# Routed attention and greedy experts on one core: one assignment product per block, split maxima in the first unit, copies on GpSimd, another order

## The chip, the cores and the metric

The kernel runs on one core of a Trainium2 chip. A core has TensorE (matrix products into PSUM), VectorE, ScalarE, GpSimd (elementwise work; GpSimd reaches SBUF only) and SyncE, which issues most of the DMAs; the profile calls them PE, DVE, ACT, POOL and SP. The metric is the device time of one execution in microseconds (us); smaller is better.

## The reference

Clustered attention feeds a layer of eight experts with a greedy, capacity-limited assignment.

```python
# q, k, v: (4, 8, 768, 64); centroids: (8, 16, 64)
q_assign = argmax(normalised(q) . normalised(c)); k_assign = argmax(normalised(k) . normalised(c))
mask = q_assign[:, :, :, None] == k_assign[:, :, None, :]
scores = where(mask, scale * q @ k.T, -1e9); scores -= max(scores, -1)
attn = exp(scores) / (sum + 1e-9);  x = (attn @ v) as (3072, 512)
logits = x @ w_gate                     # (3072, 8)
# all 24576 logits, largest first: give the token to the expert if it has none and the expert has < 384
out[mask_e] = relu(x[mask_e] @ w1[e]) @ w2[e]    # 8 experts, 512 -> 1024 -> 512
```

The argmax and the greedy order must come out as in float32, so the kernel splits most operands into a high and a low f16 part and adds their products.

## The kernel before

Attention is done in 8 units of four heads (`U = 8`, `HG = 4`); a head has 768 rows, six blocks of 128 (`J = 6`), so a unit has 24 blocks (`T = 24`). For every unit:

- `load` brings q, k and v in (SyncE's queue). `split_sc` (line 642) scales by 64, `split_hi` (646) makes the f16 high part and `split_lo` (650) the f16 remainder, called a residue here: on VectorE if its last argument is D, on GpSimd if it is P. `dup` (657) copies the high part into a second tile on ScalarE. `trans` (734) transposes by DMA on SyncE's queue; in unit 0 `pt` and `ptc` (738, 750) transpose on TensorE and copy out.
- `cent` (676) multiplies each of the 24 blocks with the unit's centroids. The centroids are also split in two, so `assign` (664) issues two matmuls of 16 columns per block, which add up in PSUM (tile `mx`). `hot0` to `hot5` (681, 697) turn the result into a one-hot mark on VectorE and write it with ScalarE beside q and k (+32768 for q, -32768 where k differs), so that a product of the marked operands is masked. Unit 0 does this head by head (`cent0`, `hh0` to `hh5`).
- `m_mm` (780) makes the masked scores of one block of queries, 2 x 384 columns, in a PSUM buffer `sc`; `m_rd` (787) takes the row maximum on VectorE. `row0` to `row2` put the maxima into the operand of the next product.
- `b_mm` (818) makes the transposed scores less the maximum, again in `sc`; `b_exp` (829) takes the exponential on ScalarE; `res` (835) makes the f16 residue of the weights, on GpSimd (P) or VectorE (D).
- `av` (850) multiplies with v: per block of 128 rows three matmuls of 66, 64 and 66 columns (`rest_of`, 840, is the third), and a fourth for the mean rows in one block of six. `out0` to `hi1` divide and split, `xst` stores, `xtr` transposes, `lg0` to `lg2` make the logits.

There are three buffers `sc`, shared by `m_mm`, `b_mm` and `pt`, and one buffer `mx`. Each engine works strictly in the order in which the instructions are issued to it, and that order is written out by hand: `ATT_ORDER` (22) is a text of some 2,050 steps such as `m_mm,3,5`, and a loop (1079) calls them one after the other. `wd` is a dummy product (671) that keeps TensorE busy, `tab,n` a step that fills a constant table (984), `tex` an exponential of one column (529) ahead of which the exponential table is loaded, `c2,n` the n-th operation of the centroids' norm (537), `bb` a first step of the routing. `FFN_ORDER` (186) does the same for routing and experts.

Of the kernel before, what the change touches and what calls it, by code (L numbers as in the profile page):

```python
# [21 lines left out]
tew teh ident load,0,q,0,A tex split_hi,0,q,0,D ones load,0,k,0 wtio wd loadc wd tab,0 misc wd tab,4 load,0,k,3 wd  # L22
load,0,k,2 wd load,0,k,1 wd load,0,q,1 split_lo,0,q,0,D load,0,q,2 pt,0,qa,0 c0 c1 load,0,v,- split_hi,0,k,0,D c2,0
load,1,k,- wd c2,1 wd c2,2 load,0,q,3 c2,3 split_sc,0,k,3 wd zkb split_lo,0,k,0,D loadg wd split_hi,0,k,3,P c2,4 wd c2,5
dup,0,k,3 c2,6 pt,0,ka,0 c2,7 split_sc,0,k,2 tab,18 c2,8 c2,9 split_hi,0,k,2,P wd c2,10 c2,11 wd split_sc,0,k,1 c2,12
c2,13 wd c2,15 c2,14 dup,0,q,0 wd ptc,0,qa,0,D c3 wd split_hi,0,k,1,P wd ptc,0,ka,0,D wd dup,0,k,1 wd split_lo,0,k,1,P
wd c4 wd dup,0,k,2 cent0,0,k split_sc,0,q,1 cent0,0,q split_lo,0,k,3,P wd split_sc,0,q,2 wd hh0,0 wd split_hi,0,q,1,P wd
hh1,0 pt,0,ka,1 tab,23 split_hi,0,q,2,P hh2,0 wd split_lo,0,q,1,P wd pt,0,ka,3 dup,0,k,0 hh3,0 dup,0,q,1 hh4,0,q hh4,0,k
split_lo,0,q,2,P pt,0,qa,1 ptc,0,ka,1,D hh5,0,k hh5,0,q wd wd split_sc,0,v,- ptc,0,qa,1,D cent0,1,k zqb tab,7 cent0,1,q
ptc,0,ka,3,D wd wd hh0,1 zqm wd split_hi,0,v,-,P pt,0,qb,0 hh1,1 pt,0,qa,2 split_lo,0,k,2,P hh2,1 pt,0,kb,0 hh3,1 wd wd  # L30
ptc,0,kb,0,D wd ptc,0,qb,0,A load,1,q,- split_lo,0,v,-,P hh4,1,q hh4,1,k ptc,0,qa,2,D split_sc,1,k,- m_mm,0,1 wd wd
m_rd,0,1 wd wd m_mm,0,0 split_sc,0,q,3 pt,0,ka,2 m_rd,0,0 m_mm,0,2 split_hi,0,q,3,P wd split_hi,1,k,-,P split_lo,0,q,3,P
m_rd,0,2 vs,0 load,1,v,- hh5,1,q split_lo,1,k,-,P ptc,0,ka,2,A wd pt,0,qb,1 wd vact,0 ptc,0,qb,1,D m_mm,0,3 vh2,0
m_mm,0,5 dup,0,q,3 vl2,0 wd wd hh5,1,k wd m_rd,0,3 dup,0,q,2 cent0,2,k cent0,2,q pt,0,kb,1 hh0,2 wd m_rd,0,5 wd
ptc,0,kb,1,A trans,1,ka,- wd wd pt,0,qa,3 split_sc,1,q,- wd hh1,2 m_mm,0,7 ptc,0,qa,3,D wd wd hh2,2 wd wd wd hh3,2 wd
split_hi,1,q,-,P m_mm,0,4 hh4,2,k hh4,2,q m_rd,0,7 cent0,3,k cent0,3,q wd hh5,2,q wd hh0,3 split_lo,1,q,-,P hh5,2,k wd
load,2,k,- m_rd,0,4 pt,0,qb,2 m_mm,0,6 ptc,0,qb,2,A wd wd hh1,3 wd m_rd,0,6 wd split_sc,1,v,- wd pt,0,kb,2 wd m_mm,0,9
hh2,3 wd hh3,3 wd wd ptc,0,kb,2,D wd wd trans,1,qa,- m_mm,0,8 hh4,3,q hh4,3,k hh5,3,q wd m_rd,0,9 split_hi,1,v,-,P
cent,1,k,0 cent,1,k,1 cent,1,k,2 m_rd,0,8 cent,1,k,3 wd hh5,3,k pt,0,qb,3 hot0,1,k m_mm,0,11 ptc,0,qb,3,A row1,0,0
row0,0,0 hot1,1,k pt,0,qm,0 m_rd,0,11 wd wd ptc,0,qm,0,A wd load,2,q,- wd wd pt,0,kb,3 hot2,1,k load,2,v,- dup,1,q,-  # L40
b_mm,0,0 ptc,0,kb,3,D m_mm,0,10 hot3,1,k wd wd m_rd,0,10 b_exp,0,0 wd wd wd m_mm,0,13 hot4,1,k res,0,0,P wd wd m_mm,0,12
m_rd,0,13 hot5,1,k cent,1,q,0 dup,1,k,- wd m_mm,0,14 m_rd,0,12 split_lo,1,v,-,P cent,1,q,1 cent,1,q,2 cent,1,q,3
m_rd,0,14 split_hi,2,k,-,D m_mm,0,15 trans,1,kb,- b_mm,0,2 m_rd,0,15 b_mm,0,1 b_exp,0,2 hot0,1,q m_mm,0,16 wd row0,0,1
b_exp,0,1 row1,0,1 wd hot1,1,q res,0,2,P wd pt,0,qm,1 m_rd,0,16 b_mm,0,3 ptc,0,qm,1,A hot2,1,q b_mm,0,5 res,0,1,P
b_exp,0,3 hot3,1,q wd m_mm,0,17 b_exp,0,5 hot4,1,q b_mm,0,4 split_lo,2,k,-,D hot5,1,q vs,1 split_hi,2,q,-,D trans,1,qb,-
wd m_rd,0,17 res,0,5,P m_mm,0,19 b_exp,0,4 wd m_rd,0,19 m_mm,0,18 b_mm,0,6 res,0,4,P m_rd,0,18 m_mm,0,20 b_exp,0,6
av,0,0 trans,2,ka,- m_mm,0,21 row1,0,2 row0,0,2 m_rd,0,20 b_mm,0,7 av,0,1 m_rd,0,21 b_exp,0,7 m_mm,0,22 split_hi,2,v,-,D
av,0,2 res,0,7,P m_rd,0,22 pt,0,qm,2 m_mm,0,23 b_mm,0,8 ptc,0,qm,2,A m_rd,0,23 tab,35 load,3,k,- res,0,3,P vact,1
b_mm,0,9 load,3,q,- vh2,1 b_exp,0,8 vl2,1 m_mm,1,0 av,0,3 m_rd,1,0 b_exp,0,9 res,0,8,P av,0,4 m_mm,1,1 av,0,5 m_rd,1,1
res,0,6,P b_mm,0,10 out0,0,0 m_mm,1,2 out1,0,0 b_exp,0,10 out2,0,0,D b_mm,0,11 res,0,9,P m_rd,1,2 hi0,0,0 cent,2,k,0  # L50
m_mm,1,4 b_exp,0,11 cent,2,k,1 cent,2,k,2 dup,2,k,- row1,0,3 tab,12 row0,0,3 hi1,0,0 res,0,10,P b_mm,0,13 m_rd,1,4
# [388 lines left out]
def routed_attention_greedy_moe(ctx: ExitStack, tc: tile.TileContext, q, k, v, centroids,  # L440
# [16 lines left out]
    BIG = 32768.0  # L457
    ER = 96
# [1080 lines left out]
```

## Time and profile before

| | |
|---|---|
| median of three runs | 676.03 us (675.4 to 678.72) |
| the profiled execution, its own time | 675.39 us |
| its span, first to last instruction | 673.6 us |
| TensorE / VectorE / ScalarE / GpSimd busy | 96% / 75% / 62% / 72% |
| mean granted TensorE clock | 0.978 of full speed |

The busy time of an engine is the time in which at least one of its instructions runs; matmuls overlap each other, so the distance from one start to the next tells more of TensorE than their durations. A line of a group reads: line of the kernel, engine, operation, output and inputs by name and shape, count, then busy time, mean duration in ns, and the idle time just before. The first product with v starts at 50.2 us in unit 0 and at 93.6, 136.1, 179.7, 220.6, 262.7, 304.9 and 343.2 us in units 1 to 7; the last one ends at 369.4 us.

### The profile page before, as it was taken

To read this page: it belongs to the slowest core of one execution; us is meant where nothing else is said; L and a number is where in the kernel's file an instruction comes from. 1 tells how busy PE (TensorE), PEld (TensorE's weight loads), DVE (VectorE), ACT (ScalarE), POOL (GpSimd) and SP (SyncE) were. 2 spreads that over 40 slices of the span, in tenths; PEclk is the share of its full clock that TensorE was granted. 3 is DMA by queue.
4 is the path that set the end of the run, shared out by engine and by line. 5 is a ranking of instruction groups with operands and counts; after the bars stand their busy time and mean duration, and the time that the engine had idled before them with its cause. 6 is when DMAs were issued, how large, how long until landed. Compare 5 with 4: busy or idle time off the path is not lost. (4 is left out here: it accounts for less than half of the span.)

```text
span 673.6 us, 19685 instructions
## 1 busy us (share of the span) xinstructions
PE 644.6 (96%) x8246; PEld 433.5 (64%) x8246; DVE 505.7 (75%) x1160; ACT 418.9 (62%) x552; POOL 484.4 (72%) x390
## 2 busy tenths in 40 slices
PE   8999999999999999999999569999999999999996
PEld 4667777776777777777777459554545454545453
DVE  6898999999998989998887687877768585822020
ACT  7886676685757767566455045849484857598121
POOL 7668889898798877977774456667795949498401
PEclk9999999999999999999999569999999999999999
DMA  6897889776996969572223053829485765796101
GB/s 191 197 205 167 163 153 231 114 179 164 169 197 132 168 178 139 98 142 55 52 50 74 26 175 130 307 92 300 150 241 208 183 251 157 264 322 164 48 1 47
DMA packets 175450, 105.84 MB, mean 157 GB/s; under 512 B 135426, under 2 KB 160002, under 8 KB 175362
## 3 DMA queue, kind: packets, MB, share of 16 engines
q1 hardware_dynamic: 171378, 91.81, 56.7%
q0 software_dynamic: 3840, 12.59, 5.2%
q8 instruction: 64, 1.05, 0.6%
q10 hardware_dynamic: 144, 0.20, 0.1%
q14 instruction: 24, 0.20, 0.1%
HBM read 58.77 MB, written 12.58 MB: 106 GB/s over the span
## 5 line engine op out<-in xcount | busy, mean ns | idle before, releaser
L838 POOL TENSOR_TENSOR rt<-pt 128x768 f16<-128x768 f32 x176 | 266.9, 1542 | 62.4 <-ACT pt L830 62.2
L830 ACT ACTIVATE pt<-sc 128x768 f32<-128x768 f32 x192 | 150.5, 811 | 102.3 <-PE sc L827 99.5
L788 DVE TENSOR_REDUCE mxs<-sc 128x1 f32<-128x768 f32 x192 | 178.7, 951 | 12.6 <-PE sc L784 11.2
L1447 PE MATMUL pf<-xgt,w1h 128*128 128x384 f16 (+1 forms) x640 | 129.6, 295 | 0.3 <-DVE xgt L1436 0.3
L860 PE MATMUL av<-vh,pt 128*128 128x66 f16 x1152 | 121.7, 194 | 0.2 <-DVE xb L893 0.2
L841 PE MATMUL av<-vh,rt 128*128 128x66 f16 x1152 | 121.4, 193 | 0.0
L862 PE MATMUL av<-vl,pt 128*128 128x64 f16 x1152 | 121.4, 191 | 0.0
L860 PEld LDWEIGHTS <-pt 128*128 128x128 bf16 x1152 | 106.0, 97 | 8.3
L862 PEld LDWEIGHTS <-pt 128*128 128x128 bf16 x1152 | 105.5, 98 | 8.7 <-issue 0.7
L841 PEld LDWEIGHTS <-rt 128*128 128x128 f16 x1152 | 104.7, 97 | 0.0
L823 PE MATMUL sc<-qbt,kbt 99*128 99x384 f16 x384 | 93.8, 325 | 1.0 <-DMA qbt<-mt 0.4
L827 PE MATMUL sc<-qat,kat 128*128 128x384 f16 x384 | 93.7, 325 | 0.0
L784 PE MATMUL sc<-kbt,qbt 80*128 80x384 f16 x384 | 90.2, 325 | 1.5 <-ACT qbt L746 0.7
L1447 PE MATMUL pf<-xgt,w1l 128*128 128x384 f16 (+1 forms) x320 | 90.5, 295 | 0.0
L1447 PEld LDWEIGHTS <-w1h 128*128 128x128 f16 x640 | 57.8, 98 | 28.5 <-issue 1.0
L1411 POOL TENSOR_TENSOR w2l<-wr,w2h 128x1024 f16<-128x1024 f32 x32 | 67.6, 2134 | 4.2 <-ACT w2h L1404 3.9
L1485 PE MATMUL pf<-w2h,hh 128*128 128x512 f16 x184 | 69.6, 378 | 0.0
L1485 PE MATMUL pf<-w2h,hl 128*128 128x512 f16 x184 | 69.4, 378 | 0.0
L1485 PE MATMUL pf<-w2l,hh 128*128 128x512 f16 x184 | 69.4, 378 | 0.0
L1401 ACT ACTIVATE wr<-wr 128x1024 f32<-128x1024 f32 x63 | 65.7, 1046 | 4.3 <-DMA wr<-in_moe_w_dram 3.6
L1411 POOL TENSOR_TENSOR w1l<-wr,w1h 128x1024 f16<-128x1024 f32 x31 | 65.4, 2136 | 0.3
L1479 DVE SCALAR_TENSOR_TENSOR hl<-pf,hh 128x384 f16<-128x384 f32 x56 | 30.7, 551 | 40.7 <-ACT hh L1476 36.6
(259 smaller groups left out, 1137.1 us busy)
## 6 DMA issues: line engine op xcount, KB each, us to landing
wr<-in_moe_w_dram SPq DMA_DIRECT2D x64, 512.0 KB
ld<-in_v_dram SPq DMA_DIRECT2D x8, 768.0 KB
xrow<-xb SPq DMA_DIRECT2D x16, 384.0 KB
ld<-in_k_dram SPq DMA_DIRECT2D x7, 768.0 KB
ld<-in_q_dram SPq DMA_DIRECT2D x7, 768.0 KB
ld<-in_k_dram SPq DMA_DIRECT2D x4, 192.0 KB
ld<-in_q_dram SPq DMA_DIRECT2D x3, 192.0 KB
xg<-xrow,idx POOLq DMA_INDIRECT x24, 6.5
```

The costliest lines, as they stand in the source:

```text
L784: nc.tensor.matmul(p[:, half, :S // 2], QBT[u][:D + C, i, :], KBT[u][:D + C, h * J + half * 3:h * J + half * 3 + 3, :], start=True, stop=True)
L788: nc.vector.tensor_reduce(mxs[u % 3][:, i:i + 1], MP.pop((u, i))[:, :, :S // 2], axis=AX.XY, op=OP.max)
L823: nc.tensor.matmul(ps[:, half, :S // 2], KBT[u][:ER + 3, s, :], QBT[u][:ER + 3, cs, :], start=True, stop=False)
L827: nc.tensor.matmul(ps[:, half, :S // 2], KAT[u][:, s, :], QAT[u][:, cs, :], start=False, stop=True)
L830: nc.scalar.activation(pts[(u * 12 + s // 2) % RP][:, s % 2], MP.pop((u, "b", s))[:, :, :S // 2], AF.Exp, scale=ESC)
L838: (nc.vector if e == "D" else nc.gpsimd).tensor_sub(rts[x][:, s % 2], p.rearrange("p a b -> p (a b)"), hi_view(pts[x])[:, s % 2])
L841: nc.tensor.matmul(o[:, j, :], r[:, j * P:(j + 1) * P], VH[u][:, s, :], start=False, stop=(s % J == J - 1), skip_group_check=True)
L860: nc.tensor.matmul(o[:, j, :], hi[:, js], VH[u][:, s, :], start=(kt == 0 and j == 0), stop=False, skip_group_check=True)
L862: nc.tensor.matmul(o[:, j, :D], hi[:, js], VL[u][:, s, :], start=False, stop=False, skip_group_check=True)
L1411: nc.gpsimd.tensor_sub(lo, wrs[c], hi)
L1447: nc.tensor.matmul(o, (w1l if i == 2 else w1h)[x][:, c, fs], xgt[x][:, h + int(i == 1), ts], start=(first and i == 0), stop=(last and i == ...
L1485: nc.tensor.matmul(PS["o", p, g], (hl if i == 2 else hh)[x][:, f, g * P:(g + 1) * P], (w2l if i == 1 else w2h)[x][:, f, :], start=(f == 0 ...
```

## The change

One text order for another, and six edits of the functions:

- `cent` makes one product of 32 columns per block, the high and the low centroids beside each other, in a buffer `sc`; a new step `hotb` (`small`) copies the low half to SBUF on ScalarE and `hota` (`both`) adds it to the high half on VectorE, into `mx`. This holds for units 1 to 7.
- In unit 0, for heads 1 to 3 (18 of the 24 blocks), `kd` forms the difference of the first three key blocks and the last three, `m_mm` multiplies the queries with the difference a - b and with b, `m_rl` takes relu(a - b) on ScalarE, and `m_rd` takes the maximum of b + relu(a - b) over 384 columns in one VectorE instruction with an accumulator.
- `av` and `rest_of` multiply 65 columns of v instead of 66.
- The centroids' norm takes 10 VectorE operations instead of 16.
- `dup` and `split_sc` can run on GpSimd. The order does so for six duplicates of one head in unit 0, two of four heads in unit 1, and the scaling of v in unit 0 and of k, q and v in unit 1.
- Of the `res` steps, ten that were on VectorE go to GpSimd, and eight the other way.

```diff
     def cent(u, name, h):
         if h == 0:
+            PC["w", name] = psc.tile([P, T, 2, C], F32, name="sc")
+        if h == 1:
             PC[name] = pmx.tile([P, T, C], F32, name="mx")
-        assign(PC[name][:, h * J:(h + 1) * J], (QAT if name == "q" else KAT)[u], u % NG, h, h == 0)
+        o, src, g = PC["w", name], (QAT if name == "q" else KAT)[u], u % NG * HG + h
+        for j in range(h * J, (h + 1) * J):
+            nc.tensor.matmul(o[:, j], src[:, j, :], ct[:, :, g * C:(g + 1) * C], start=(j % 16 == 0), stop=True,
+                             skip_group_check=True)
+
+    def small(u, name):
+        nc.scalar.activation(cb, PC["w", name][:, :, 1], AF.Copy)
+
+    def both(u, name):
+        nc.vector.tensor_tensor(PC[name], PC.pop(("w", name))[:, :, 0], cb, op=OP.add)
...
         for half in range(2):
-            nc.tensor.matmul(p[:, half, :S // 2], QBT[u][:D + C, i, :],
-                             KBT[u][:D + C, h * J + half * 3:h * J + half * 3 + 3, :], start=True, stop=True)
+            x = KBT[u][:D + C, h * J + half * 3:h * J + half * 3 + 3, :]
+            if paired(u, i) and half == 0:
+                x = kdv(h)
+            nc.tensor.matmul(p[:, half, :S // 2], QBT[u][:D + C, i, :], x, start=True, stop=True)
+
+    def paired(u, i):
+        return u == 0 and i >= 1 * J
...
+    def kd(u, h):
+        k = KBT[u][:D + C, h * J:(h + 1) * J, :]
+        nc.vector.tensor_sub(kdv(h), k[:, 0:3], k[:, 3:6])
+
+    def m_rl(u, i):
+        nc.scalar.activation(rlv(i), MP[u, i][:, 0, :S // 2], AF.Relu)
 
     def m_rd(u, i):
-        nc.vector.tensor_reduce(mxs[u % 3][:, i:i + 1], MP.pop((u, i))[:, :, :S // 2], axis=AX.XY, op=OP.max)
+        o, p = mxs[u % 3][:, i:i + 1], MP.pop((u, i))
+        if paired(u, i):
+            nc.vector.tensor_tensor_reduce(rlv(i), p[:, 1, :S // 2], rlv(i), 1.0, LOWEST,
+                                           op0=OP.add, op1=OP.max, accum_out=o)
+        else:
+            nc.vector.tensor_reduce(o, p[:, :, :S // 2], axis=AX.XY, op=OP.max)
...
-            nc.tensor.matmul(o[:, j, :], hi[:, js], VH[u][:, s, :], start=(kt == 0 and j == 0), stop=False,
+            nc.tensor.matmul(o[:, j, :D + 1], hi[:, js], VH[u][:, s, :D + 1], start=(kt == 0 and j == 0), stop=False,
...
-    def split_sc(u, name, hh):
+    def split_sc(u, name, hh, e="A"):
         src, hi, lo = parts(u, name, hh)
+        if e == "P":
+            nc.gpsimd.tensor_scalar(src, src, SQ, None, op0=OP.mult)
+            return
...
-    def dup(u, name, hh):
+    def dup(u, name, hh, e="A"):
         ts = cols(hh)
+        if e == "P":
+            x, y = (qb[:, ts, 0:D], qa[:, ts, 0:D]) if name == "q" else (kb[:, ts, 0:D], ka[:, ts, D:])
+            nc.gpsimd.tensor_copy(x, y)
+            return
...
-    chain(ts, ss[:, 1:2], ss[:, 1:2], 1e-30, None, op0=OP.max)
-    for _ in range(2):
-        chain(nc.vector.reciprocal, ss[:, 2:3], ss[:, 1:2])
-        chain(nc.vector.tensor_mul, ss[:, 2:3], ss[:, 2:3], ss[:, 0:1])
-        chain(nc.vector.tensor_add, ss[:, 1:2], ss[:, 1:2], ss[:, 2:3])
-        chain(ts, ss[:, 1:2], ss[:, 1:2], 0.5, None, op0=OP.mult)
+    chain(ts, s0, s0, 1e-30, None, op0=OP.max)
+    chain(nc.vector.reciprocal, r0, s0)
+    chain(stt, s0, r0, n0, s0, op0=OP.mult, op1=OP.add)
...
```

Of the order, the start before and after, and the assignments of unit 7 after:

```diff
-tew teh ident load,0,q,0,A tex split_hi,0,q,0,D ones load,0,k,0 wtio wd loadc wd tab,0 misc wd tab,4 load,0,k,3 wd
...
+m_rd,6,2 cent,7,k,1 cent,7,k,2 res,5,7,P cent,7,k,3 hi0,5,0 b_mm,5,11 hotb,7,k hi1,5,0 m_mm,6,4 hota,7,k b_exp,5,11
```

In the new order `load,0,q,0,A` is followed by `ones`, `zqb` and `load,0,k,1`; `tew`, `teh` and `ident` come some 20 steps later and `tex` behind the first `m_rl`. `load,2,k` comes ahead of unit 1's first transposes. Up to the first `av` there are 91 dummy products in both orders.

## Rows read from the trace of the kernel before

**Rows 1.** The page, busy time, share of span and instructions of each engine.
```profile
PE 644.6 (96%) x8246; PEld 433.5 (64%) x8246; DVE 505.7 (75%) x1160; ACT 418.9 (62%) x552; POOL 484.4 (72%) x390
```

**Rows 2.** Busy time by stretch: from:to, length, then busy us and count per engine.
```profile
0.00:50.20 50.20, 44.80 (x487) 29.53 (x488) 41.66 (x96) 41.63 (x62) 33.51 (x46) 1.00 0.81 198
50.20:93.60 43.40, 42.91 (x738) 32.41 (x736) 40.73 (x66) 30.05 (x40) 36.77 (x29) 1.00 0.84 176
93.60:136.10 42.50, 41.73 (x733) 31.60 (x732) 40.16 (x67) 28.58 (x38) 35.54 (x27) 1.00 0.80 159
136.10:179.70 43.60, 42.23 (x734) 31.83 (x733) 41.37 (x67) 28.37 (x38) 38.83 (x29) 1.00 0.80 165
179.70:220.60 40.90, 40.90 (x729) 31.44 (x728) 38.01 (x63) 28.24 (x37) 35.76 (x26) 1.00 0.80 171
220.60:262.70 42.10, 41.86 (x734) 31.77 (x732) 38.33 (x63) 28.65 (x38) 35.09 (x26) 1.00 0.90 172
262.70:304.90 42.20, 42.20 (x738) 32.17 (x736) 39.85 (x67) 26.30 (x37) 34.79 (x28) 1.00 0.63 119
304.90:343.20 38.30, 38.30 (x626) 28.18 (x624) 31.77 (x54) 21.26 (x31) 30.36 (x22) 1.00 0.20 36
343.20:369.40 26.20, 26.20 (x548) 21.17 (x546) 20.56 (x39) 14.86 (x22) 14.44 (x10) 1.00 0.39 79
```

**Rows 3.** TensorE in order of time: start us, us, engine, line, operation, count.
```profile
124.81 0.45 PE L667 MATMUL mx<-ct,qat 128*128 128x16 f16 x12
125.11 0.49 PE L823 MATMUL sc<-qbt,kbt 99*128 99x384 f16 x2
125.44 0.49 PE L827 MATMUL sc<-qat,kat 128*128 128x384 f16 x2
```

**Rows 4.** TensorE in order of time, 36 products with v and the next product.
```profile
279.83 0.19 PE L860 MATMUL av<-vh,pt 128*128 128x66 f16 x1
...
280.91 0.49 PE L823 MATMUL sc<-qbt,kbt 99*128 99x384 f16 x2
```

**Rows 5.** Waits from 50.2 to 343.2: who for whom, us, times, longest.
```profile
DVE mxs L788 <- PE sc L784: 11.0, 21, 1.9
```

**Rows 6.** Groups by line over the span: the assignment products, one product with v.
```profile
L860 PE MATMUL av<-vh,pt 128*128 128x66 f16 x1152 | 121.7, 194 | 0.2 <-DVE xb L893 0.2
L667 PE MATMUL mx<-ct,qat 128*128 128x16 f16 x384 | 13.3, 169 | 1.3 <-DVE L L964 1.3
L667 PE MATMUL mx<-ct,kat 128*128 128x16 f16 x384 | 12.9, 169 | 0.9 <-DVE ceq L700 0.6 <-DVE vm L775 0.2
```

**Rows 7.** Groups of ScalarE, 0 to 100 us: a copy from PSUM, the table load.
```profile
L889 ACT ACTIVATE xb<-av 128x384 f16<-128x384 f32 x4 | 2.0, 489 | 1.3 <-DVE av L881 1.3
L530 ACT ACT_TABLE_LOAD x1 | 1.3, 1283 | 1.2 <-PEq L1525 1.2
```

**Rows 8.** VectorE in order of time, around maxima and mark steps.
```profile
38.94 3.54 DVE L788 TENSOR_REDUCE mxs<-sc 128x1 f32<-128x768 f32 x4
42.40 0.55 DVE L689 TENSOR_REDUCE cmx<-mx 128x24 f32<-128x384 f32 x1
...
43.12 0.55 DVE L691 TENSOR_TENSOR mx<-mx,cmx 128x384 f32<-128x384 f32 x1
43.59 0.94 DVE L788 TENSOR_REDUCE mxs<-sc 128x1 f32<-128x768 f32 x1
```

**Rows 9.** VectorE in order of time, in the centroids' norm.
```profile
5.07 0.08 DVE L518 DVE_READ_ACCUMULATOR sq<-cf 128x1 f32 x1
...
6.29 0.17 DVE L538 RECIPROCAL ss<-ss 128x1 f32<-128x1 f32 x1
```

**Rows 10.** Groups of GpSimd: two copies (365 to 480 us), a subtraction (0 to 100).
```profile
L1225 POOL COPY rep<-pick 128x128 f16<-128x128 f16 x1 | 0.3, 287 | 0.1
L1378 POOL COPY eg<-ei 1x1 int32<-1x1 int32 x1 | 0.2, 177 | 0.0
...
L655 POOL TENSOR_TENSOR vl<-ld,vh 128x1536 f16<-128x1536 f32 x2 | 6.0, 2988 | 0.7 <-ACT vh L648 0.7
```

More of the change, by code (lines that the diff above doesn't have):

```diff
@@ L27 @@
[L27 to L41, printed above, removed]
@@ L47 @@
[L47 to L51, printed above, removed]
@@ L182 @@
-res,7,22,D av,7,20 av,7,21 res,7,23,D av,7,22 av,7,23 lg1,7,0 avr,22 lg2,7,0 avr,23 out0,7,3 out1,7,3 out2,7,3,D hi0,7,3
-h1h,0 h1h,1 xpt,0,0 xpc,0,0,A xpt,0,1 xpt,1,0 xpc,0,1,A xpc,1,0,D xst,7,1 xpt,1,1 lgh,0,0 xpc,1,1,D lgh,1,0 lgh,0,1
-bb,0,4 lga,1 lgh,1,1 lga,0 bb,1,0 bb,1,5 bb,1,1 bb,1,6 bb,1,2 bb,1,8 bb,1,3 bb,1,9 bb,1,4 bb,1,10
+load,0,q,0,A ones zqb wd load,0,k,1 loadc tab,0 wtio tab,4 load,0,k,0 misc load,0,k,3 load,0,q,1 load,0,k,2
+split_sc,0,k,1 load,0,q,2 split_hi,0,q,0,D load,0,v,- load,0,q,3 c0 load,1,k,- tew teh split_hi,0,k,0,D split_hi,0,k,1,P
@@ new lines @@
+av,1,9 b_mm,1,12 split_lo,3,v,-,D load,4,q,- m_mm,2,5 b_exp,1,12 b_mm,1,14 av,1,10 hot2,3,k res,1,12,P b_exp,1,14
+av,1,11 m_rd,2,5 b_mm,1,15 out0,1,1 hot3,3,k res,1,13,P b_mm,1,16 b_exp,1,15 out1,1,1 hot4,3,k m_mm,2,7 out2,1,1,D
+b_exp,1,16 b_mm,1,17 res,1,15,P m_rd,2,7 hi0,1,1 m_mm,2,8 b_exp,1,17 lg0,0,1 hi1,1,1 b_mm,1,18 m_rd,2,8 res,1,14,P
+xtr,1,0 m_mm,2,10 b_exp,1,18 av,1,12 lg1,0,1 m_rd,2,10 m_mm,2,9 dup,3,k,- res,1,16,P m_mm,2,11 load,4,v,- av,1,13
+m_rd,2,9 m_mm,2,13 split_hi,4,k,-,D m_rd,2,11 res,1,17,P av,1,14 b_mm,1,19 m_rd,2,13 hot5,3,k av,1,15 b_exp,1,19
@@ L185 @@
+bb,1,4
 """
@@ L626, in routed_attention_greedy_moe @@
     rc = st.tile([P, J], F32, name="rc")
+    cb = st.tile([P, T, C], F32, name="cb")
     def cols(hh):
@@ L840, in rest_of @@
     def rest_of(o, r, u, s, j):
-        nc.tensor.matmul(o[:, j, :], r[:, j * P:(j + 1) * P], VH[u][:, s, :], start=False, stop=(s % J == J - 1),
+        nc.tensor.matmul(o[:, j, :D + 1], r[:, j * P:(j + 1) * P], VH[u][:, s, :D + 1], start=False, stop=(s % J == J - 1),
                          skip_group_check=True)
@@ L865, in av @@
             if kt == 1:
-                nc.tensor.matmul(o[:, j, :], QBT[u][:, h * J + j, :], vms[u % 3][:, h, :], start=False, stop=False,
+                nc.tensor.matmul(o[:, j, :D + 1], QBT[u][:, h * J + j, :], vms[u % 3][:, h, :D + 1], start=False, stop=False,
                                  skip_group_check=True)
@@ L1076, in routed_attention_greedy_moe @@
               lg2=lg2, loadc=load_c, loadg=load_g, ident=identity, wtio=rank, zqb=zero_q, zkb=zero_k, misc=fills, ones=ones, c0=norm0,
-              c1=norm1, tex=table, tew=zero_w, teh=half_w, c3=norm3, c4=norm4, wgs=gate_split)
+              c1=norm1, tex=table, tew=zero_w, teh=half_w, c3=norm3, c4=norm4, hotb=small, hota=both, wgs=gate_split)
     steps = tables()
@@ L1083, in routed_attention_greedy_moe @@
             norm2[args[0]]()
-        elif name[:3] == "hot":
+        elif name[:3] == "hot" and name[3] < "6":
             hots(int(name[3]), *args)
```

323 lines of the change are left out of this document (176 added, 147 removed).

## Prediction

> **What bounds the kernel now.** I read the page's busy shares first: TensorE 96%, VectorE 75%, ScalarE 62%, GpSimd 72% [rows 1]. That is an average over two different halves, so the next view is the busy time by stretch, cut where each unit's first product with v starts [rows 2]. The reader is to see three things there. Attention ends at 369.4 us, and the other 304.2 us of the span (routing and experts) hold nothing that the change touches. In the stretches from 50.2 to 304.9 TensorE is never idle for more than 1.4 us of some 42, and VectorE is busy 38.0 to 41.4 us of the same 42. The first 50.2 us are another regime: VectorE and ScalarE are both busy for about 41.7 us, and TensorE's 44.8 contain dummy products that nobody waits for.
>
> TensorE's busy time overlaps itself, since a matmul lasts longer than its distance to the next, so the third view is the order of time on TensorE. Twelve 16-column assignment products start within 0.30 us, from 124.81 to the next line at 125.11: 25 ns each. A pair of 384-column products takes 0.33 us, 0.163 each [rows 3]. The 36 products with v between 279.83 and 280.91 take 30 ns each [rows 4]. A stretch of 733 matmuls (93.6 to 136.1) is 143 wide ones (23.3 us), 458 with v (13.7), 96 for the assignments and 24 for the gate (3.0) and 12 column sums of 256 columns (1.3 by their columns): 41.3 us of 42.5. The six full stretches have 729 to 738 matmuls, so each has a floor of about 41 us on TensorE.
>
> Their lengths, though, follow VectorE. With 40.2 to 41.4 us of VectorE work they took 42.5 to 43.6 us, with 38.0 to 38.3 only 40.9 to 42.1 [rows 2]. Two engines are loaded to within 2 to 4 us of the stretch and pass the same three PSUM buffers to each other; VectorE's longest idle time is for maxima whose scores are not there yet, 11.0 us in 21 waits [rows 5]. Whoever lightens one engine alone gets part of it.
>
> **The change, part by part.**
>
> *One product per block.* For units 1 to 7 each block's two 16-column products become one of 32 columns. The two lines show 384 matmuls each [rows 6]; 48 of each are unit 0's, which keeps its own routine, so 672 become 336. The 32-column form is not in the trace; it lies between the 16-column 25 ns and the 66-column 30 ns. At 25 ns the saving is 336 x 25 = 8.4 us, at 30 ns 6.7 us. I take 8.4, as the pitch hardly moves from 16 to 66 columns. The Trainium skill says in "TensorE: Matmul & The Clock Gate" (Part 1) that start-to-start never drops below about 25 ns however small the product is, with 25 ns at 32 columns; the trace agrees at 16.
>
> What it adds: per unit and name one ScalarE copy of 128x384 and one VectorE add of 128x384 that reads PSUM and the copy. The copy goes by the nearest ScalarE row, 489 ns [rows 7], 14 x 0.49 = 6.8 us, hidden: ScalarE is busy at most 30 of 43 us per stretch [rows 2]. The add goes by the like operation on the assignments, which starts at 43.12 with its successor at 43.59: 0.47 us [rows 8]; bounds 0.47 and 0.55 (its whole duration). 14 x 0.47 = 6.6 us on VectorE. The add waits for the copy, and the next maximum stands behind it on VectorE; one to three steps lie between the two in the order. If a 0.8 us exponential is ahead of the copy on ScalarE, VectorE stands still for up to that: 0 to 14 x 0.8. I take 0 for most and keep the rest for the range. The product now also takes one of the three score buffers: 2 holders more beside 48 per unit, for about as long; I take 0, bound 14 x 0.5 us.
>
> *65 columns for 66.* The two products with v whose weights carry the ones column, 1152 each [rows 6], and the mean rows' (one in six of 1152) lose a column. At 30 ns per 66 columns that is at most 0.45 ns each, 1.1 us; at least 0 (the pitch has a floor). I take 1.0.
>
> *Maxima of heads 1 to 3 of unit 0.* A 768-wide maximum costs 0.865 us from start to start (four from 38.94 to 42.40) [rows 8]. In its place stand a ScalarE relu of 384 and a VectorE add-and-maximum of 384. The latter is not in the trace: below, 0.47 us plus 0.08 for reading an accumulator [rows 9], 0.55; above, 0.87 plus 0.08. I take 0.60, nearest to the two-input row: 18 x 0.265 = 4.8 us off VectorE, at the other end 1.4 more. Three key differences of 384 f16 come in at about 0.3 us (bounds 0.2 and 0.47): +0.9. The relus load ScalarE with 18 x 384 elements; it sheds 6 x 384 + 6 x 1536 by the duplicates and scalings that leave it, so ScalarE is not worse off.
>
> *Norm chain.* 16 small VectorE operations become 10; one is 0.17 us [rows 9] and about 0.19 with its wait: -1.1 us at the start of VectorE's chain.
>
> *To GpSimd.* Six duplicates of 384, two of 1536, four scalings of 1536. GpSimd's one-input price by rows: 177 ns for one element, 287 ns for 128 [rows 10], that is 0.87 ns per element; so 0.51 and 1.51 us, 12.1 us in all. Upper end is its two-input subtraction, 2.99 us per 1536 [rows 10]: 24 us. GpSimd is busy 33.5 of the first 50.2 us [rows 2], part of the rest being wait for ScalarE, so 12 us fit, barely; 24 do not.
>
> *Order.* Counting the order's steps up to the first product with v, VectorE loses 3.7 (14 of the 18 maxima lie there), 1.1 (chain) and 1.7 (one long residue of q or k now comes later), and gains 0.9 (differences), 0.95 (unit 1's two adds), 0.87 (a residue moved from GpSimd) and 1.3 (table steps that came forward): -2.4. Behind it, VectorE has 12 adds (+5.6), one long residue (+1.7), three residues of weights fewer (-2.6), four cheaper maxima (-1.1) and fewer table steps (-1.3): +2.4. TensorE has 7.2 (six units' products) and 1.0 less there. The exponential table load goes from the very start, where ScalarE had no data yet, to behind the first relu: 1.28 us [rows 7] if it is issued there, 0 if the load stays first; I take 0.3. Loads are issued in another order on SyncE's queue (unit 2's k earlier, before the first transposes); the first 50 us have 0.81 DMA share [rows 2]; +-0.5.
>
> The Trainium skill's "ScalarE: Activation LUTs" (What ACT_TABLE_LOAD costs) prices each switch of the table set at about 2.66 us with its drain; the load of 1283 ns agrees with the row, the drain no run here shows. By that the sum would be up to 2.4 us higher.
>
> *Sum.* The first product with v starts 2.4 us earlier (VectorE sets it). From there to 369.4 TensorE would give 8.2 us and VectorE would take 2.4. In 319.2 us VectorE is busy 290.8 us by the eight stretches of [rows 2] and TensorE about 309 (six times 41, then 37 and 26 by their counts of matmuls); afterwards about 293 and 301. The stretches followed both engines, so I take the middle of -8.2 and +2.4: -2.8. With +0.3 for the table: -2.4 - 2.8 + 0.3 = -4.9. The profiled execution took 675.39 us (673.6 of span, 1.8 around it), 0.6 below the median of the three runs, 676.03. Forecast 670.5.
>
> **Rivals.**
> 1. *TensorE alone decides.* For it: it is idle less than anyone in every stretch [rows 2], and quicker scores shorten VectorE's 11.0 us of waits [rows 5]. Against: lengths follow VectorE. Time: -2.4 - 8.2 = -10.6, 664.8.
> 2. *VectorE alone decides.* The adds put back what the maxima and the order take off: -2.4 + 2.4, and its idle time stays as it is: 675.4, no change. For it: the correlation of the stretches; its load per middle unit rises by 0.95 us while TensorE's falls by 1.35. Against: part of its idle time is wait for TensorE.
> 3. *GpSimd becomes the bound of the opening (slower).* The duplicates and scalings run at the two-input price. GpSimd then has 33.5 + 20 (24 less the steps of it that moved later) = 54 us of work, still waits for ScalarE now and then (4 us of its 16.7 us idle time now), and the first product with v comes at 58 instead of 50.2. Later the sum is -2.8 as before: 675.4 + 7.8 - 2.8 = 680.4. It decides from about 2.2 us per 1536 elements on. For it: GpSimd's 12 us barely fit. Against: 0.87 ns per element between its two copy rows. The Trainium skill's "GPSIMD Engine Reference" (4.1 Engine selection) advises against elementwise work there, about twice VectorE's time for two inputs, but calls one input roughly line-rate; by the first half this rival comes true, by the second it does not, and the copy rows side with the second.
>
> **How the numbers follow.** Forecast (668 to 673) 0.45; rival 1 0.20; rival 2 0.20; rival 3 0.15. What a measurement here can tell from no change is 0.5%, 3.4 us. Faster by more than that (under 672.6): 0.36 of the forecast's 0.45, 0.20, and 0.02 of rival 2, 0.58. Same: 0.09, 0.16 and 0.02: 0.27. Slower: the rest of rivals 2 and 3, 0.15. The range reaches from rival 1's time to beyond rival 2's, 664.5 to 678; it leaves out most of rival 3 and the tail below rival 1.
>
> **What would show it.** Right, if the 32-column products start 25 ns apart; if VectorE's add-and-maximum has a pitch of about 0.6 us; if a GpSimd scaling of 1536 lasts about 1.5 us; if the first product with v starts near 48 us, and the stretches between first products shorten by less than 1 us while TensorE's idle time in them grows. If they shorten by 1.3 us each, rival 1; if VectorE is busy 97% of them at the old length, rival 2; a GpSimd without a gap up to 55 us is rival 3. Wrong altogether, if the time past the end of attention is not 304 us as before.

## The result and the profile after

The changed kernel takes 686.11 us (median of 4 runs, 685.39 to 687.39), the kernel before 675.96 in the same comparison: a ratio of 1.0141, 95% interval 1.0121 to 1.0160. It is slower by 10 us; forecast were 670.5 us, faster, with a range that ended at 678. The profiled span is 684.3 us instead of 673.6.

The view to start from is the busy time by stretch, cut again where each unit's first product with v starts (from:to, length, then busy us and count of PE, PEld, DVE, ACT, POOL, granted clock, DMA share, GB/s), of the changed kernel:

```profile
0.00:66.70 66.70, 48.60 (x439) 31.25 (x440) 51.20 (x112) 36.53 (x65) 52.74 (x57) 0.90 0.57 149
66.70:108.90 42.20, 41.64 (x686) 31.08 (x685) 39.50 (x72) 32.39 (x46) 37.70 (x28) 1.00 0.80 157
108.90:150.00 41.10, 40.75 (x686) 30.40 (x685) 40.14 (x66) 30.62 (x39) 34.04 (x25) 1.00 0.81 178
150.00:191.30 41.30, 41.26 (x692) 31.02 (x690) 39.83 (x68) 28.93 (x40) 38.99 (x29) 1.00 0.89 187
191.30:232.10 40.80, 40.80 (x683) 30.45 (x682) 38.95 (x65) 29.85 (x39) 36.55 (x27) 1.00 0.86 178
232.10:272.80 40.70, 40.70 (x687) 30.63 (x685) 38.34 (x64) 29.70 (x40) 34.49 (x25) 1.00 0.70 146
272.80:314.20 41.40, 41.29 (x688) 30.73 (x687) 38.23 (x67) 26.91 (x38) 37.16 (x29) 1.00 0.72 124
314.20:351.00 36.80, 36.78 (x620) 27.45 (x618) 30.88 (x54) 19.42 (x29) 30.73 (x23) 1.00 0.27 58
351.00:379.50 28.50, 28.02 (x559) 22.11 (x558) 23.84 (x41) 16.42 (x24) 17.22 (x14) 1.00 0.38 73
```

Against [rows 2] the change splits into two effects of opposite sign. The first stretch has grown from 50.2 to 66.7 us, and in it GpSimd's busy time from 33.5 to 52.7, ScalarE's has shrunk from 41.6 to 36.5. From there to the last product with v the kernel is quicker: 312.8 us instead of 319.2. What follows attention is as long as before (684.3 - 379.5 = 304.8 us, 304.2 before). So +16.5 - 6.4 + 0.6 = +10.7 us of span.

What fills GpSimd in the opening is in its groups (line, operation, out<-in, shapes, count | busy us, mean ns of one | idle before):

```profile
L652 POOL TENSOR_SCALAR ld<-ld 128x1536 f32<-128x1536 f32 x4 | 16.4, 4096 | 0.0
L665 POOL TENSOR_TENSOR vl<-ld,vh 128x1536 f16<-128x1536 f32 x2 | 6.0, 2984 | 0.3 <-ACT vh L658 0.3
...
L671 POOL COPY qb<-qa 128x384 f16<-128x384 f16 x3 | 1.9, 621 | 0.0
L671 POOL COPY kb<-ka 128x384 f16<-128x384 f16 x3 | 1.5, 495 | 0.0
L671 POOL COPY kb<-ka 128x1536 f16<-128x1536 f16 x1 | 1.5, 1462 | 3.2 <-PE sc L767 3.2
L671 POOL COPY qb<-qa 128x1536 f16<-128x1536 f16 x1 | 1.5, 1462 | 0.0
```

The duplicates (L671) cost what the copies of [rows 10] had promised, 0.50 to 0.62 us and 1.46 us. The scalings (L652) cost 4.10 us each, more than the two-input residues (L665, 2.98), although they read one input.

A scaling does not only delay GpSimd's own queue. Three engines in order of time around the last of the four, and the same VectorE line later (start us, us, engine, line, operation; in brackets the idle time before and what ended it), of the changed kernel:

```profile
40.27 4.12 POOL L652 TENSOR_SCALAR ld<-ld 128x1536 f32<-128x1536 f32 x1
...
40.28 0.17 DVE L851 TENSOR_SCALAR qm<-mxs 128x12 f16<-128x12 f32 x1
40.35 4.07 DVE L855 TENSOR_SCALAR qm<-mxs 128x12 f16<-128x12 f32 x1
43.46 0.96 DVE L826 TENSOR_TENSOR xb<-kbt 80x384 f16<-80x384 f16 x1
43.73 1.14 DVE L834 CUSTOM_DVE_ANT_0 xt<-sc,xt 128x384 f32<-128x384 f32 x1
...
57.38 0.17 DVE L855 TENSOR_SCALAR qm<-mxs 128x12 f16<-128x12 f32 x1
...
40.13 0.61 PE L697 MATMUL sc<-ct,kat 128*128 128x32 f16 x18
40.59 0.32 PE L688 MATMUL av<-onesh 128*128 128x384 f16 x1
40.75 0.30 PE L697 MATMUL sc<-ct,kat 128*128 128x32 f16 x6
44.57 0.85 PE L767 MATMUL sc<-ident,qm 128*100 128x128 f16 x6 [3.52 <-POOL wdig L1045]
```

A VectorE operation on 12 elements per partition, 0.17 us long at 57.38 us, where no GpSimd instruction runs beside it, lasts 4.07 us and ends within 0.04 us of the scaling. (The line above it is the like operation; it starts within 0.01 us of the scaling and is not held.) The transposes of its result are next on TensorE, which stands still from 41.05 to 44.57; after that it runs at the lower of its two clocks, 1.2 GHz (0.85 us for six transposes that took 0.49 at 38.00); the granted clock is 0.66 on average between 40 and 50 us, and 0.90 over the whole opening. Before, it was 1.00 throughout the opening [rows 2]. The bracket names another instruction of GpSimd that happened to end there; the operands say that the wait is for qm.

### The profile page after: what moved, and what is told of

Read it like the earlier page. It is cut to its first block, busy times and chain, and to the rows that moved or that the text cites. A ratio compares the mean times of both kernels' runs of the same rounds, so it can differ in the third digit from the quotient of the medians.

```text
span 684.3 us, 19099 instructions
## 1 busy us (share of the span) xinstructions
PE 643.5 (94%) x7910; PEld 428.5 (63%) x7910; DVE 513.9 (75%) x1187; ACT 422.0 (62%) x572; POOL 508.8 (74%) x404
## 5 line engine op out<-in xcount | busy, mean ns | idle before, releaser
L837 DVE TENSOR_REDUCE mxs<-sc 128x1 f32<-128x768 f32 x174 | 161.1, 950 | 11.7 <-PE sc L812 10.4
L909 PE MATMUL av<-vh,pt 128*128 128x65 f16 x1152 | 122.7, 194 | 0.5 <-DVE xb L942 0.5
L890 PE MATMUL av<-vh,rt 128*128 128x65 f16 x1152 | 122.1, 193 | 0.0
L812 PE MATMUL sc<-kbt,qbt 80*128 80x384 f16 x366 | 87.0, 326 | 0.7 <-ACT qbt L771 0.4
```

The costliest lines, as they stand in the source:

```text
L812: nc.tensor.matmul(p[:, half, :S // 2], QBT[u][:D + C, i, :], x, start=True, stop=True)
L837: nc.vector.tensor_reduce(o, p[:, :, :S // 2], axis=AX.XY, op=OP.max)
L890: nc.tensor.matmul(o[:, j, :D + 1], r[:, j * P:(j + 1) * P], VH[u][:, s, :D + 1], start=False, stop=(s % J == J - 1), skip_group_check=True)
L909: nc.tensor.matmul(o[:, j, :D + 1], hi[:, js], VH[u][:, s, :D + 1], start=(kt == 0 and j == 0), stop=False, skip_group_check=True)
```

## The experiments

Theory 1: GpSimd's work (four times 4.1 us) sets the opening. Theory 2: VectorE stands still while GpSimd's long instructions run, so that the length of one counts beside their sum. Theory 3: the paired maxima or the order are to blame. Later theories came from the results. "First" is the start of the first product with v; "middle" is from there to the end of the last one, both in the profiled execution. (The end is that of the products of the weights' high part with v; the third products end about 0.4 us later in every run.) Single executions of one run differ by up to 6 us (e2 from 681.3 to 686.0, e3 from 679.6 to 685.8), and first and middle come from one of them.

```
run                what it is                                      first  middle  median  ratio to before (95%)
before                                                              50.2   319.2   676 to 678
after                                                               66.7   312.8   686.11  1.0141 (1.0121-1.0160)
e1_scale_scalar    after, scalings on ScalarE                       58.2   313.4   677.94  1.0005 (0.9989-1.0021)
e2_dup_scalar      after, duplicates on ScalarE                     64.4   313.2   683.24  1.0078 (1.0048-1.0108)
e3_scale_pieces    after, each scaling in four pieces               61.2   312.9   682.35  1.0073 (1.0047-1.0098)
e4_unpaired        after, no paired maxima                          64.8   314.4   686.02  1.0127 (1.0092-1.0161)
e5_old_opening     new operations, old opening, new later order     54.7   313.6   676.12  0.9991 (0.9977-1.0006)
e6_old_order       new operations, old order                        55.9   335.8   697.86  1.0304 (1.0285-1.0323)
e7_before_scale    before, scalings on GpSimd                       61.5   320.0   688.44  1.0177 (1.0157-1.0197)
e8_none            after, scalings + duplicates back, no pairs      56.4   313.5   675.59  0.9985 (0.9970-0.9999)
e9_old_opening_two e5, unit 1 with two products per block           49.8   315.7   670.53  0.9897 (0.9872-0.9922)
e10_new_order_two  e8, unit 1 with two products per block           56.2   314.3   676.04  0.9975 (0.9959-0.9992)
e11_two_input      after, other forms of scaling                    63.6   312.8   683.12  1.0084 (1.0052-1.0116)
e12_paired_only    after, scalings + duplicates back                56.3   312.8   676.25  0.9983 (0.9963-1.0002)
e13_old_start      old order to the first maximum, then new         54.0   314.0   673.95  0.9956 (0.9932-0.9979)
e14_new_start      new order to the first maximum, then old         53.0   314.9   673.17  0.9939 (0.9915-0.9962)
```

**The scalings back on ScalarE.**
```diff
-split_sc,0,v,-,P   split_sc,1,k,-,P   split_sc,1,q,-,P   split_sc,1,v,-,P
+split_sc,0,v,-     split_sc,1,k,-     split_sc,1,q,-     split_sc,1,v,-
```


> The kernel after the change, with its four 128x1536 scalings back on ScalarE; the order of steps and all else unchanged. Theory 1 (GpSimd's work: a scaling lasts 4.1 us there, 16.4 us in all, and the splits and transposes of unit 1 stand behind it): GpSimd is relieved by 16.4 us, ScalarE takes 4 x 1.47 = 5.9 us, the first product with v starts at 50 to 53 us instead of 66.7, total 669 to 673. Theory 2 (VectorE stands still while GpSimd's long instructions run): the four long instructions are gone here too, so about the same. Theory 3 (the paired maxima or the order itself hold up the opening): little changes, first product with v beyond 62 us, total above 681.

First came at 58.2: 8.5 us of the 16.5 are the scalings, and nearly as many again are something else. Theories 1 and 2 had the direction and half of the size; part of theory 3 is left.

**The duplicates back on ScalarE, the scalings still on GpSimd.**
```diff
-dup,0,k,1,P   (and seven more)
+dup,0,k,1
```


> The kernel after the change, with its eight duplicates back on ScalarE and the four scalings still on GpSimd. Theory 1: GpSimd loses only 6 x 0.5 + 2 x 1.46 = 6 us, and the scalings decide; if every microsecond of GpSimd counts, first product with v at 61 us, total about 680; if the copies fill its waits for ScalarE, 684 to 686. Theory 2 (VectorE stands still behind long GpSimd instructions): the copies are short, total 684 to 686. Theory 3: no change, 686.

64.4, 2.3 us earlier, in an execution of 685.2 us; the median, 683.2, lies between the two forms of theory 1.

**Each scaling in four pieces.**
```diff
-nc.gpsimd.tensor_scalar(src, src, SQ, None, op0=OP.mult)
+for h in range(HG):
+    x = src[:, h * J:(h + 1) * J]
+    nc.gpsimd.tensor_scalar(x, x, SQ, None, op0=OP.mult)
```


> The kernel after the change, each GpSimd scaling of 128x1536 cut into four of 128x384 in a row, one per head: the same elements on the same engine at the same place of the order. Theory 1: GpSimd's time is the same (four times about 1.05 us), the first product with v stays at 65 to 68 us, total 685 to 688. Theory 2: VectorE's small operations, which last 2.5 to 4.1 us beside a long scaling, now wait for a piece of at most 1.1 us; some 8 us of VectorE come back, first product with v at 59 to 62 us, total 679 to 682. Theory 3: no change, 686.

First at 61.2, 5.5 us earlier, with more work on GpSimd; by the medians the gain is 3.8 us (686.11 to 682.35). Groups of GpSimd and VectorE in the opening of this run:

```profile
L654 POOL TENSOR_SCALAR ld<-ld 128x384 f32<-128x384 f32 x16 | 18.3, 1170 | 0.0
...
L828 DVE TENSOR_TENSOR xb<-kbt 80x384 f16<-80x384 f16 x3 | 2.1, 686 | 0.0
L1040 DVE TENSOR_SCALAR offs<-ji 128x32 f32<-128x32 int32 x4 | 1.5, 390 | 2.3 <-POOL ji L1043 2.3
L857 DVE TENSOR_SCALAR qm<-mxs 128x12 f16<-128x12 f32 x2 | 0.3, 165 | 0.0
```

The same groups of the changed kernel, whole scalings:

```profile
L826 DVE TENSOR_TENSOR xb<-kbt 80x384 f16<-80x384 f16 x3 | 6.3, 2085 | 0.0
L1038 DVE TENSOR_SCALAR offs<-ji 128x32 f32<-128x32 int32 x4 | 4.5, 1377 | 2.3 <-POOL ji L1041 2.3
L855 DVE TENSOR_SCALAR qm<-mxs 128x12 f16<-128x12 f32 x2 | 4.2, 2118 | 0.0
```

GpSimd works 1.9 us longer on the scalings and VectorE is held 11 us less on three small groups (15.0 to 3.9). Theory 1 alone allows no gain here, so theory 2 is shown: a good part of the loss is the length of one GpSimd instruction, not the sum. What follows from a held VectorE, such as TensorE's waits and lower clock (0.90 in the opening, 0.94 with pieces), is in the same 5.5 us and was not taken apart.

**Without the paired maxima.**
```diff
-        return u == 0 and i >= 1 * J
+        return False
```
with the steps `kd` and `m_rl` taken out.

> The kernel after the change, with the maxima of heads 1 to 3 of unit 0 taken as before (one 768-wide maximum on VectorE, no key differences, no relus); scalings and duplicates still on GpSimd. Theory 1: VectorE gets 18 x 0.3 = 5.4 us more in unit 0, but GpSimd sets the opening: first product with v at 65 to 70 us, total 685 to 690. Theory 2: the key differences, which last up to 2.7 us beside a scaling, are gone, but the others remain: 683 to 688. Theory 3: first product with v back near 50 us, total 671 to 676.

64.8 and no change in the total: the pairs are not what theory 3 took them for. The 1.9 us that the opening gains, the middle loses (314.4 for 312.8).

**The scalings alone, in the kernel before.**
```diff
-split_sc,0,v,-     split_sc,1,k,-     split_sc,1,q,-     split_sc,1,v,-
+split_sc,0,v,-,P   split_sc,1,k,-,P   split_sc,1,q,-,P   split_sc,1,v,-,P
```


> The kernel before, with nothing changed but four scalings of 128x1536 (unit 0's v, unit 1's k, q and v) moved from ScalarE to GpSimd. Theory 1 (GpSimd's work): 4 x 4.09 = 16.4 us come on top of its 33.5 busy of the first 50.2 us, and it had 16.7 us free in waits: unit 1's transposes and unit 0's residues of weights come late, first product with v at 56 to 62 us, total 682 to 688. If its waits take the scalings in (the rest of the change is to blame): first product with v below 53 us, total 675 to 679.

61.5 and 688.44, theory 1's upper ends. This one edit makes the old kernel slower by 1.8%, more than the whole change does. Its groups and waits of the first 61.5 us (engine, line waited for: us, times, longest):

```profile
L645 POOL TENSOR_SCALAR ld<-ld 128x1536 f32<-128x1536 f32 x4 | 16.3, 4087 | 0.0
...
ACT vh L651 <- POOL ld L645: 6.9, 2, 3.5
POOL rt L841 <- ACT pt L833: 5.9, 2, 5.6
ACT ka L651 <- POOL ld L645: 5.8, 1, 5.8
```

ScalarE saves 5.9 us of work and waits 12.7 us for the scaled data, with the rest of its queue behind it.

**The order and the other operations.**
```diff
 (e8: scalings and duplicates on ScalarE, paired() False)
 (e5: the same with the steps up to av,0,0 in the order before;
  hotb and hota of a unit stand together there, right ahead of hot0)
 (e6: the same with the order before throughout)
```


> The kernel after the change with its own order of steps throughout, but scalings and duplicates on ScalarE and the maxima of unit 0 on VectorE alone (no key differences, no relus). With the scalings alone on ScalarE the first product with v stood at 58.2 us. If the new order of the opening costs the other 8 us: still 56 to 60 us, total 675 to 679. If the paired maxima (VectorE waits for relus, key differences wait behind GpSimd) and the duplicates cost it: 50 to 53 us, total 669 to 672.

> The kernel after the change with the opening of the kernel before: its order of steps up to the first product with v, scalings and duplicates on ScalarE, maxima of unit 0 on VectorE alone; one product per block, 65 columns and the shorter norm chain stay, and so does the new order behind that point. Theory 4 (all of the loss is in the opening, all of the gain behind it): first product with v at 49 to 52 us, from there to the last one 313 us as in the changed kernel, total 668 to 672. If the later gain needs the new opening (work that it brings forward), the later part is 316 to 319 us and the total 672 to 677.

> As the run with the old opening, but the whole order of attention is that of the kernel before, with the two new steps (copy and add) put right behind a unit's last assignment product; so only the operations differ from before: one product per block for units 1 to 7, 65 columns, the shorter norm chain. If the operations bring the gain behind the opening: from first to last product with v 312 to 315 us, total 669 to 672. If it takes the new order too: 316 to 320 us, total 674 to 678; above 678 if VectorE stands still at the add for the copy.

(The old opening of e5 also holds ten steps, seven of them table steps, that the new order has ahead of its first product with v.) The first came out by the order's branch: with none of the moved work and no pairs the opening still ends at 56.4. The second missed by 3 us at the first product and hit behind it (313.6). The third came out by its last branch, far above it: the middle grew by 16.6 us although TensorE had fewer products. What the last two have in common is the copy and the add, one right behind the other. ScalarE and VectorE in order of time in the run with the old opening, and a wait of the one with the old order (55.9 to 365.4 us):

```profile
41.40 1.48 ACT L658 ACTIVATE ka<-ld 128x1536 f16<-128x1536 f32 x1
42.82 0.81 ACT L879 ACTIVATE pt<-sc 128x768 f32<-128x768 f32 x1
43.53 0.48 ACT L701 ACTIVATE cb<-sc 128x384 f32<-128x384 f32 x1
...
44.05 0.57 DVE L704 TENSOR_TENSOR mx<-sc,cb 128x384 f32<-128x384 f32 x1 [1.26 <-ACT cb L701]
...
45.19 1.44 DVE L855 TENSOR_SCALAR qm<-mxs 128x12 f16<-128x12 f32 x1
```
```profile
DVE mx L705 <- ACT cb L702: 8.2, 10, 1.3
```

The copy stands behind a 1.48 us split and an exponential on ScalarE, and VectorE waits 1.26 us at the add; with the order before it does so ten times, 8.2 of the 16.6 us. The other half is VectorE's own work: in that middle it is busy 299.2 us, 8.4 more than before (290.8), and the group with the adds alone takes 20.2 us instead of 13.4. In the changed kernel's own order the same wait sums to 0.4 us behind the opening. So the new order behind the opening is what makes one product per block pay: it gives a middle of 313.6 us, where the order before, with copy and add put in at this one place, gives 335.8. Part of that order are the 18 residues that it puts on the other engine; behind the opening VectorE has three residues of weights fewer by it (12.7 us for 16.7). No run has the new order with two products per block in every unit, so what the order would give by itself stays open.

**Two products in unit 1.**
```diff
 def cent(u, name, h):
+    if u == 1:
+        if h == 0:
+            PC[name] = pmx.tile([P, T, C], F32, name="mx")
+        assign(PC[name][:, h * J:(h + 1) * J], (QAT if name == "q" else KAT)[u], u % NG, h, h == 0)
+        return
```


> As the run with the old opening, but unit 1's assignment products are two of 16 columns as before (no copy and no add in the opening); units 2 to 7 keep one product per block and the new order. In the run with the old opening VectorE took its 17th maximum at 47.0 us and not at 43.6 as before, just when unit 1's copy and add stood there. Theory 5 (the two small steps and the score buffer that they hold cost 4 us where the engines have no room): first product with v at 49.5 to 51 us, total 669 to 672. If the shorter norm chain or the moved table steps cost it: still 54 to 55 us, total 674 to 677.

> The kernel after the change with its own order, scalings and duplicates on ScalarE, maxima of unit 0 on VectorE alone (first product with v at 56.4 us so far), and unit 1's assignment products two of 16 columns as before. If the copy and add in the opening cost the 6 us: first product with v at 50 to 52 us, total 669 to 672. If the new order of the opening costs them: 55 to 57 us, total 674 to 677.

Theory 5 held for the old opening: 54.7 became 49.8, and this kernel takes 670.53 us, ratio 0.9897 to before, faster than both kernels. (That this is nearly the forecast's 670.5 is chance: it has neither the pairs nor the work on GpSimd nor the new opening.) The lines above show a part of how the two small steps cost 4.9 us: behind them the 12-element operation at 45.19 falls beside a residue of weights on GpSimd (the second of two, 43.71 to 46.61 us together) and lasts 1.44 us, TensorE waits 2.04 us for it, and the granted clock from 45 to 50 us is 0.66; with two products in unit 1 it is 1.00. For the new order the other branch held (56.4 to 56.2): there the copy and the add have room, and the order itself costs 56.2 - 49.8 = 6.4 us.

**Only the pairs.** (Scalings and duplicates on ScalarE, all else as changed.)

> The kernel after the change with its own order, scalings and duplicates on ScalarE, but the paired maxima of unit 0 kept. Without the pairs the first product with v came at 56.4 us, with pairs and with the duplicates on GpSimd at 58.2 us. If the pairs save what VectorE's durations say (some 13 maxima by 0.3 us, less 3 differences): 53 to 55 us, total 672 to 674. If VectorE's waits for the relus and the differences behind GpSimd eat it: 57 to 59 us, total 676 to 679.

56.3 against 56.4 without pairs: they save nothing in the opening, although VectorE is busy 40.0 us of it instead of 44.2. Neither branch had it. Between 18 us and the first product VectorE waits 2.7 us for the relus (the longest 1.6) and 1.3 for the copy.

**The form of the scaling.**
```diff
+if u == 0 or name == "q":
+    nc.gpsimd.tensor_tensor(src, src, c64.to_broadcast([P, T, D]), op=OP.mult)
+else:
+    nc.gpsimd.tensor_scalar(src, src, c64[:, 0], None, op0=OP.mult)
```


> The kernel after the change with other forms of the four GpSimd scalings: unit 0's v and unit 1's q as a two-input multiplication by a column of 64s spread over the row, unit 1's k and v by a tensor-scalar operation whose factor is read from memory. It asks whether 4.09 us is the price of the operation or of the 128x1536 float elements. If of the elements: all four at 4.0 us or more, total 684 to 688. If of the operation: the two-input form at 3.0 us as the residues, first product with v at 64 to 66 us, total 683 to 686.

Its groups of GpSimd:

```profile
L657 POOL TENSOR_SCALAR ld<-ld,c 128x1536 f32<-128x1536 f32 x2 | 8.3, 4162 | 0.0
L655 POOL TENSOR_TENSOR ld<-ld,c 128x1536 f32<-128x1536 f32 x2 | 5.5, 2744 | 0.0
```

It is the operation: the same product of the same elements takes 2.74 us as a two-input multiplication and 4.16 as tensor-scalar. Two cheaper scalings (2.7 us) bring the first product 3.1 us forward.

**Half of the order each.** (Both with scalings and duplicates on ScalarE, no pairs, two products in unit 1; the seam is the first maximum.)

> Scalings and duplicates on ScalarE, maxima of unit 0 on VectorE alone, unit 1's assignment products two of 16 columns; steps up to the second row block's maximum (the first one taken) in the order before the change, from there in the new one. With the old opening throughout the first product with v came at 49.8 us, with the new one at 56.2 us, and its first maximum 2.7 us later than before. If the new order's start (other loads first, norm chain later) costs the 6.4 us: 50 to 51.5 us, total 670 to 672. If what follows the first maximum costs them: 53.5 us or more, total 673 to 677.

> The counterpart: the new order up to that first maximum, the old one from there to the first product with v, all else as in the other run. If the start costs the 6.4 us: 55 to 57 us, total 674 to 677. If the rest of the opening costs them: 50 to 53 us, total 670 to 673. If each costs a part and the parts add up, the two runs' delays over 49.8 us sum to 6.4 us.

Both halves cost: the new order behind the first maximum 54.0 - 49.8 = 4.2 us, its start 3.2; 7.4 together where both at once cost 6.4. (The seam also shifts six dummy products: 97 and 85 ahead of the first product with v instead of 91.) The start shows in VectorE's first maximum (the runs with the old opening and with the new order, both with two products):

```profile
17.93 2.80 DVE L842 TENSOR_REDUCE mxs<-sc 128x1 f32<-128x768 f32 x3 [0.31 <-PE sc L817]
```
```profile
20.18 1.82 DVE L842 TENSOR_REDUCE mxs<-sc 128x1 f32<-128x768 f32 x2
```

Which single steps of either half do it was not tried.

## Why the prediction was wrong, point by point

**The step that failed** is the price of a scaling in "To GpSimd": "0.87 ns per element; so 0.51 and 1.51 us, 12.1 us in all". Duplicates 6.4 us and scalings 16.4 make 22.8, close to the upper end of 24 of which the text itself says that it does not fit. The copies of [rows 10] were taken as the nearest rows for every one-input operation; for a copy that held, for tensor-scalar on floats it did not (2.67 ns per element), and the residue row, 2.99 us, was nearer and still too low. What that work would do to the opening the prediction put at nothing ("12 us fit, barely"); the scalings alone cost 8.5 us of it (66.7 to 58.2), 11.3 in the kernel before (50.2 to 61.5). Rival 3 named a part of the mechanism, and its condition (from about 2.2 us per 1536 elements) was met by the scalings, but not its sign, a GpSimd without a gap up to 55 us: GpSimd stands idle 3.2 us up to 47.7 and 6.8 us up to 58.9. Its 680.4 was too low because it had neither a held VectorE nor the order's cost in it. The order of the steps put each scaling ahead of a split on ScalarE, and VectorE behind it. The sums themselves are off by little: the opening's terms give -2.5, VectorE's behind it +2.3, and the forecast by them would be 670.3.

**A cost that no step had**: VectorE held by GpSimd. The prediction said what waits for a scaling's result, not what waits while it runs. The row is the 4.07 us beside 0.17; the experiment with pieces gives it 5.5 us of the opening in one execution, 3.8 by the medians. The Trainium skill states it in "SBUF — State Buffer" (Who interferes with whom): the two engines share a pair of ports, which VectorE uses in its two-port modes and for a second input from SBUF, and "Whoever issues first gets the shared pair for the whole instruction". The 4.07 us agree. The key difference at 23.19 us agrees only in part: it lasts 2.55 us and ends 0.66 us before the scaling at 22.33 to 26.40 does. Not every VectorE operation is held: a 768-wide maximum out of PSUM at 21.46 us beside a residue took 0.95 us as always, and two operations on PSUM at 31.59 and 31.98 us beside the scaling of 31.06 to 35.15 took 0.35 and 0.37 us as always.

**"The first product with v starts 2.4 us earlier (VectorE sets it)"**: the second step that failed. Taking the parts back one after the other, the first product goes 66.7 (changed), 58.2 (scalings), 56.3 (duplicates), 56.4 (pairs), 56.2 (unit 1's copy and add), 49.8 (order); the last 0.4 us against before's 50.2 are all that is left for the shorter norm chain, forecast at 1.1, and no run has it alone. The count of VectorE's work was a fair account of its busy time (40.0 us with the pairs and without the work on GpSimd, where 41.7 less 2.4 were forecast) and not of the end of the opening: the pairs, counted at -3.7 + 0.9, gave 0, since each maximum now passes through ScalarE (2.7 us of waits for the relus; the rest was not followed); the order, counted by VectorE's work alone, cost 6.4. What a part costs depends on what else is there: the scalings cost 8.5 us in the new order and 11.3 in the old one.

**One product per block: right.** 18 of them start in 0.46 us (40.13 to 40.59), 25.6 ns each. **Add-and-maximum: right**, 0.47 to 0.48 us from start to start, below the 0.60 taken, with nothing gained for it in the opening. **65 columns for 66: a term too many.** 21 products with v start between 294.63 and 295.26 us, 30 ns each as before, and over some 1,850 pairs of starts the wider products stand 30.5 ns from the next where they stood 30.6; the 1.0 us is not there. **The copy: right**, 490 ns, but "I take 0 for most" of the wait behind it is a property of the order: 0.4 us in the new one, 8.2 in the old one. **The table load: a term too many.** The load is still ScalarE's first work, 1.28 us, and the 0.3 us fall away.

**Behind the opening: the sign right, the size low**, -6.4 where -2.8 was taken as the middle of two engines. The step that failed here is taking the middle. VectorE is busy 289.7 us, as much as before (290.8) where 2.4 more were counted. The six full stretches took 247.5 us instead of 254.7, 1.2 each and 7.2 in all, which is the price of six units' 48 products at 25 ns; TensorE's idle time in them fell from 2.9 to 1.1 us, where the forecast's sign was that it grows. The seventh stretch is 1.5 shorter and the last one 2.3 longer. So this half came out near rival 1 (-8.2, of which 1.0 for the columns is missing; its sign was 1.3 each), but only with the new order: with the order before, lighter TensorE work went with 16.6 us more.

## What to carry to other kernels

Price an operation on GpSimd by a row of that very operation and type; where there is none, the bounds themselves are guesses: here the price lay beyond the far one (4.10 us against 2.99), and a scaling cost more than a two-input product. Work on GpSimd is not free because GpSimd has room: ask what VectorE issues while one long instruction runs, and keep such instructions short. A saving that passes through another engine, such as an add that needs a copy, is worth what the order leaves between the two: here another order, with some residues on another engine, took one product per block from 16.6 us of loss to 5.6 of gain.

## What was not expected of the hardware

A GpSimd tensor-scalar operation on 128x1536 floats takes 4.10 us with a constant and 4.16 with a factor from memory, a two-input multiplication by a spread column 2.74, a copy of f16 1.46. VectorE's operation on 128x12 elements took 4.07 us while such a scaling ran, 1.44 us beside a residue of weights, and 0.17 us by itself. In the opening of the changed kernel TensorE's granted clock averaged 0.66 of 2.4 GHz between 40 and 50 us, with 3.5 us of idle time in them; with the duplicates and scalings back on ScalarE it was 1.00 up to the first product. How much of the opening the lower clock itself cost was not separated.
